# A fixed order up to the first channel-mixing output, and the scores of a head pair in one run

## The chip, the core and the metric

The kernel runs on one core of a Trainium2 chip. The core's engines each take their own queue of instructions in order: TensorE (PE; matrix products and transposes, written to PSUM), VectorE (DVE), ScalarE (ACT) and GpSimd (POOL, which here only issues loads). SyncE (SP) issues the stores. The metric is the device time of one execution in microseconds (us); for the kernel before it is the median of 11 runs, 346.16 us.

## The reference

Inputs are float32: q, k, v of 8 batches x 8 heads x 576 positions x 64, and four weight matrices. First comes sliding-window attention with a bias linear in distance, then an MLP mixer over its output.

```python
rel  = pos[:, None] - pos[None, :]
mask = (rel >= 0) & (rel < 128)
scores = where(mask, q @ k.T / sqrt(64) - slope[h] * abs(rel), -1e9)
x = softmax(scores) @ v                 # heads side by side: (8, 576, 512)
h = maximum(x.T @ w_tok1, 0) @ w_tok2   # token mixing: 576 -> 256 -> 576
u = x + h.T
out = u + maximum(u @ w_ch1, 0) @ w_ch2 # channel mixing: 512 -> 1536 -> 512
```

Each query sees itself and the 127 positions before it, so only the diagonal blocks of scores and their neighbours are computed.

## The kernel before

**Attention** goes by head pairs: g counts them over all batches, four to a batch, 0 to 31. A pair has three steps.

- `att_T(g)`: twelve transposes (L201) from the regrouped copies qg and kg into one PSUM tile tT, then a copy of q by ScalarE (L210) and of k by VectorE (L211) into qT and kT. For batch 0 (`early`) both copies are ScalarE's.
- `att_S(g, half)`: score products of half of the key blocks into a PSUM tile sp (L233: four matmuls in half 0, six in half 1, each using 64 of the array's 128 rows), two exponentials by ScalarE into pe (L241), and one product with the mask by VectorE into pb (L245).
- `att_V(g)`: eighteen matmuls with v into a PSUM tile ot (L267; v has a column of ones, which gives the sum), a reciprocal rt (L274) and the scaled copy into xb (L275).

tT, sp and ot share the PSUM pool `ps_at`, which has two buffers of two banks each. pe has three buffers, pb nine.

`regroup(b, h0, h1)` (L142) reorders the loaded q and k of a batch on VectorE, into qg and kg. It reads qn and kn, which `dma_qk` loads through POOL's queue, and it must come before the batch's `att_T`. The regroup of batch b+1 is called at the end of `att_T` of batch b's last pair (from batch 1 on), followed by `dma_qk(b + 3)`. `att_V` of a batch's last pair issues the loads of v for batch b+2.

**The mixer** of a batch has five steps. `tok1` is two groups of five matmuls (t, L310), with ScalarE's ReLU r1t (L315). `tok2` is five groups of two (ht, L323), with VectorE's addition ub (L327). `trans_u` is four groups of five transposes (ut, L336 and L340), with VectorE's copies UT (L345). `ch1` is 24 tiles ct of four matmuls (L351), each with ScalarE's ReLU into R2 (L356). `ch2` is four or five output chunks of twelve matmuls (o2, L379), cut into three parts of four; VectorE adds ub (L391) or copies (L387), and SP stores. All of these use the PSUM pool `ps_ma`, which has four buffers of one bank.

**The order.** `mixer_items(b, lead)` lists the work of mixer b together with the ch2 chunks of batch b-1: `lead` chunks stand before `tok1`, one behind it, one between the parts of `tok2`, the rest around `trans_u`. Every item has a cost written by hand. `spread(main, side)` calls the main items in order and puts the side items among them in proportion to these costs; `att_step(g)` gives the side items T(g+2), S(g+1) twice, V(g).

Three stretches follow each other:

1. Attention of batch 0, in an order written out by hand (`tc.manual_schedule()`: it holds for all engines).
2. Mixer 0, spread with attention of batch 1 (`att_step` from g = 2 on, limited to g >= 4 by `g0`; since it reaches ahead, T(8), T(9) and S(8) fall in here too) and with the first three ch2 chunks of batch 0 (`lead=3`, n1 = 9 parts). Here and after it, only TensorE's order is as called (`engines={ENG.PE}`). For the other engines the framework's scheduler sets the order. `regroup(1, 0, H)` is called as a side item of cost 0, behind the first twelve of the ch1 tiles of mixer 0.
3. Mixers 1 to 8, each spread with the attention of the batch after it.

The functions and the main part:

Of the kernel before, what the change touches and what calls it, by code (L numbers as in the profile page):

```python
# [9 lines left out]
ACT = mybir.ActivationFunctionType  # L10
ALU = mybir.AluOpType
ENG = mybir.EngineType
# [26 lines left out]
def kernel(  # L39
# [11 lines left out]
    nc = tc.nc  # L51
    P = nc.NUM_PARTITIONS
    B, H, S, D = q.shape
# [3 lines left out]
    scale = 1.0 / math.sqrt(D)  # L57
    slopes = [2.0 ** (-8.0 * (h + 1) / H) for h in range(H)]
    bf16 = mybir.dt.bfloat16
    f32 = mybir.dt.float32  # L60

    assert (S, D, H, B % 2) == (576, 64, 8, 0)
    NF = S // P
    TAIL = S - NF * P
    NCH = NF + 1
    W0 = S - P
    NHP = H // 2
    NDH = DTOK // P
    NCB = DM // P
    NHT = DCH // P  # L70
# [7 lines left out]
    pepool = ctx.enter_context(tc.tile_pool(name="pe", bufs=3))  # L78
    pbpool = ctx.enter_context(tc.tile_pool(name="pb", bufs=9))
# [5 lines left out]
    ps_at = ctx.enter_context(tc.tile_pool(name="ps_at", bufs=2, space=bass.MemoryType.PSUM))  # L85
# [21 lines left out]
    biascol = const.tile([P, H], f32, name="biascol")  # L107
# [3 lines left out]
    masks = const.tile([P, 2, H, 512], bf16, name="masks")  # L111


    def dma_qk(b, h0, h1):
        for raw, src in ((qn, q), (kn, k)):
            nc.gpsimd.dma_start(
                out=raw[b % 2][:RP, h0:h1, :],
                in_=src[b, h0:h1, :, :].rearrange("h (p j) d -> p h (j d)", j=TPP),
            )
# [70 lines left out]
    pbs = {}  # L190
# [23 lines left out]
            if b + 3 < B:  # L214
                dma_qk(b + 3, 0, H)

    def att_S(g, half):
        b, hp = divmod(g, NHP)
        qt, kt = qT[g % NR], kT[g % NR]
        sp = ps_at.tile([P, 2, 512], f32, name="sp", tag="at")  # L220
        for i in range(2):
            kb = 2 * half + i
            lastp = kb == NF - 1
            w = P + TAIL if lastp else 2 * P

            mms = [(0, w, kb * P, kb * P)]
            if lastp:
                mms.append((w, 2 * P, W0, NF * P))
            for x0, x1, k0, q0 in mms:

                for hh in range(2):
                    r = slice(hh * D, (hh + 1) * D)
                    nc.tensor.matmul(  # L233
                        sp[:, hh, i * 256 + x0 : i * 256 + x1],
                        lhsT=kt[r, k0 : k0 + P], rhs=qt[r, q0 : q0 + x1 - x0],
                        start=True, stop=True,
                    )
        pe = pepool.tile([P, 2, 512], bf16, name="pe", tag="pe")
        for i in range(2):
            h = 2 * hp + i  # L240
            nc.scalar.activation(  # L241
                out=pe[:, i, :], in_=sp[:, i, :], func=ACT.Exp, bias=biascol[:, h : h + 1], scale=scale,
            )
        pb = pbpool.tile([P, 2, 512], bf16, name="pb", tag="pb")
        nc.vector.tensor_tensor(  # L245
            out=pb[:, :, :], in0=pe[:, :, :],
            in1=masks[:, half, 2 * hp : 2 * hp + 2, :], op=ALU.mult,
        )
        pbs[g, half] = pb

    def att_V(g):
        b, hp = divmod(g, NHP)
# [34 lines left out]

    NG = B * NHP

    def att_step(g, g0=0):  # L290

        its = []
        if g0 <= g + 2 < NG:
            its.append((0.6, lambda: att_T(g + 2)))
        if g0 <= g + 1 < NG:
            its.append((0.5, lambda: att_S(g + 1, 0)))
            its.append((0.5, lambda: att_S(g + 1, 1)))
        if g0 <= g < NG:
            its.append((0.6, lambda: att_V(g)))
        return its  # L300

# [95 lines left out]
    def mixer_items(b, lead=1):  # L397

        chunks = []
        if b > 0:  # L400
            cs = list(range(NF)) if (b - 1) % 2 == 0 else [NF] + list(range(NF))
            chunks = [ch2_items(b - 1, c) for c in cs]
        its = []
        for _ in range(lead if chunks else 0):
            its += chunks.pop(0)
        if b < B:
            its += [(1.07, lambda dh=dh: tok1(b, dh)) for dh in range(NDH)]
            if chunks:
                its += chunks.pop(0)
            mid = chunks.pop(0) if chunks else []  # L410
            for c in range(NCH):
                its.append((0.43, lambda c=c: tok2(b, c)))
                if mid and c % 2 == 0:
                    its.append(mid.pop(0))
            its += mid
            last = chunks.pop() if chunks else []
            for ch in chunks:
                its += ch
            its += last[:1]
            for cb in range(NCB):  # L420
                its.append((0.25, lambda cb=cb: trans_u(b, cb)))
            its += last[1:]
            for ht_i in range(NHT):
                for x in range(2):
                    its.append((0.48, lambda ht_i=ht_i, x=x: ch1(b, ht_i, x)))
        else:
            for ch in chunks:
                its += ch
        return its


    with tc.manual_schedule():
        for i in range(2):
            nc.vector.memset(vp[i][:, :, :, D : D + 1], 1.0)
            nc.vector.memset(vp[i][0 : P - TAIL, NF, :, 0:D], 0.0)
        nc.vector.memset(W1[0 : P - TAIL, NF, :], 0.0)
        nc.vector.memset(patT[0 : P - TAIL, :], 0.0)
        dma_qk(0, 0, 2)
        nc.gpsimd.iota(
            row[:, :], pattern=[[1, P]], base=0, channel_multiplier=0,  # L440
            allow_small_or_imprecise_dtypes=True,
        )
        nc.gpsimd.iota(
            pidx, pattern=[[0, 1]], base=0, channel_multiplier=1,
            allow_small_or_imprecise_dtypes=True,
        )
        for hp in range(1, NHP):
            dma_qk(0, 2 * hp, 2 * hp + 2)
        dma_v_tail(0)
        for h in range(H):  # L450
            dma_v_head(0, h)
        nc.gpsimd.dma_start(
            out=W1[:, 0:NF, :], in_=moe_w_tok1[0 : NF * P, :].rearrange("(c p) d -> p c d", p=P)
        )
        nc.gpsimd.dma_start(out=W1[P - TAIL : P, NF, :], in_=moe_w_tok1[NF * P : S, :])
        nc.gpsimd.dma_start(
            out=W2[:, :, :], in_=moe_w_tok2.rearrange("(j p) s -> p j s", p=P)
        )
        for n in range(3):
            cs = slice(n * DCH // 3, (n + 1) * DCH // 3)  # L460
            nc.gpsimd.dma_start(
                out=WC1[:, :, cs], in_=moe_w_ch1[:, cs].rearrange("(j p) h -> p j h", p=P)
            )
        dma_qk(1, 0, H)
        nc.gpsimd.dma_start(
            out=WC2[:, :, :], in_=moe_w_ch2.rearrange("(j p) c -> p j c", p=P)
        )
        dma_v_tail(1)
        for c in range(NF):
            dma_v(1, c)  # L470


        build_consts()
        regroup(0, 0, 2)
        build_bias()
        att_T(0, True)
        build_masks(0)
        regroup(0, 2, 4)
        att_S(0, 0)
        att_T(1, True)  # L480
        build_masks(1)
        att_S(0, 1)
        regroup(0, 4, 6)
        att_S(1, 0)
        att_T(2, True)
        build_masks(2)
        att_S(1, 1)
        regroup(0, 6, 8)
        if B > 2:
            dma_qk(2, 0, H)  # L490
        att_S(2, 0)
        att_T(3, True)
        build_masks(3)
        att_S(2, 1)
        att_V(0)
        att_S(3, 0)
        att_V(1)
        att_S(3, 1)
        att_V(2)
        att_V(3)  # L500
        nc.vector.tensor_copy(out=swap[:, 0:TAIL], in_=ident[:, TAIL:P])
        nc.vector.tensor_copy(out=swap[:, TAIL:P], in_=ident[:, 0:TAIL])

    def run(its):
        for _, f in its:
            f()

    with tc.manual_schedule(engines={ENG.PE}):

        its0, its1 = mixer_items(0), mixer_items(1, lead=3)  # L510
        n0, n1 = len(its0) - NHT, 9
        run(its0[:n0])
        side = [(0.0, lambda: regroup(1, 0, H))]
        if B > 3:
            side.append((0.0, lambda: dma_qk(3, 0, H)))
        for g in range(NHP - 2, 2 * NHP):
            side += att_step(g, NHP)
        spread(its0[n0:] + its1[:n1], side)
        side = []
        for g in range(2 * NHP, 3 * NHP):  # L520
            side += att_step(g)
        spread(its1[n1:], side)
        for b in range(2, B + 1):
            side = []
            for g in range(NHP * (b + 1), NHP * (b + 2)):
                side += att_step(g)
            spread(mixer_items(b), side)
# [30 lines left out]
```

The softmax here doesn't subtract the row's maximum and nothing guards it: scores larger than these inputs give would overflow.

## Time and profile before

| | us |
|---|---|
| median of 11 runs (lowest, highest) | 346.16 (343.89, 348.07) |
| profiled execution: its time | 346.83 |
| its span, first to last instruction | 345.0 |
| TensorE matmuls busy | 306.7 (89%) |
| VectorE busy | 180.4 (52%) |
| ScalarE busy | 179.0 (52%) |
| GpSimd busy | 59.1 (17%) |
| mean of one: exponential L241 / ReLU L356 | 0.696 / 0.425 |
| mean of one: mask product L245 / regroup copy of a batch L142 | 0.689 / 0.95 |

Rows of a timeline give start, duration, engine, line, operation, out<-in with shapes, count, and in brackets the idle time before it with what ended it. A duration reaches from start to the end of the writes, and the next instruction on the same engine can start before that; what one costs in a row of many is the distance of starts. Rows of a waits view give engine, line and tile, what it waited for, us in total, times and the longest. Slices cut the span in 40; a digit is the busy share in tenths.

### The profile page before, as it was taken

Reading aid. Unit: us, or ns where it says so; the run is one execution under the profiler, and the core shown is the slowest. Engines: PE = TensorE matmul, PEld = TensorE weight load, DVE = VectorE, ACT = ScalarE, POOL = GpSimd, SP = SyncE. Lnnn points to the kernel's source line nnn. Section 1 sums busy time; section 2 is a strip of 40 time slices with the busy share of each in tenths; the row PEclk is TensorE's granted clock in tenths of the full one; section 3 lists DMA queues with packets and bytes.
Section 4 is the critical chain, followed back from the end, with each engine's and each line's share of the span. In section 5 each row is a group of like instructions: output and inputs, shape, how many; then the busy total and the mean of one; then the engine's idle time right before and its main releaser. Section 6 shows DMA issues by size and latency. Waiting matters only on the chain.

```text
span 345.0 us, 6712 instructions
## 1 busy us (share of the span) xinstructions
PE 306.7 (89%) x2816; PEld 189.3 (55%) x2816; DVE 180.4 (52%) x342; ACT 179.0 (52%) x373; POOL 59.1 (17%) x79
## 2 busy tenths in 40 slices
PE   2570689997789999999999999999999999999995
PEld 1350257553377545765567546764576456746742
DVE  6861452774864478434952396346932573335012
ACT  3850139854449643784369533855396427612800
POOL 8963150104100410022100400040000000000000
PEclk9999999998989999999999999999999999999999
DMA  7999999699190849109750902075000210011022
GB/s 89 136 171 205 199 165 148 85 195 99 33 137 2 56 75 194 39 4 98 118 112 2 99 32 86 7 49 83 33 32 2 61 61 32 2 61 63 0 63 92
DMA packets 59502, 27.76 MB, mean 80 GB/s; under 512 B 38672, under 2 KB 54864, under 8 KB 59472
## 3 DMA queue, kind: packets, MB, share of 16 engines
q0 software_dynamic: 54224, 17.90, 53.5%
q1 hardware_dynamic: 5248, 9.44, 8.2%
q8 instruction: 22, 0.36, 0.5%
q14 instruction: 8, 0.07, 0.1%
HBM read 35.78 MB, written 9.44 MB: 131 GB/s over the span
## 4 chain that ended last, share of the span: by engine, by line
PE 74%; DVE 10%; DMA 6%; POOL 3%; ACT 3%; issue 2%; ACTq 0%; POOLq 0%
PE ct L351 27%; PE o L379 24%; PE t L310 6%; DMA kn<-in_k_dram 6%; PE sp L233 4%; PE ot L267 4%; PE tT L201 3%; DVE ub L327 3%; PE ht L323 2%; PE ut L340 2%; DVE kg L142 2%; ACT pe L241 2%; POOL vp L134 2%; DVE kT L211 1%; DVE xb L275 1%
## 5 line engine op out<-in xcount | busy, mean ns | idle before, releaser
L379 PE MATMUL o<-WC,R 128*128 128x512 bf16 x432 | 104.2, 379 | 0.0
L351 PE MATMUL ct<-UT,WC 128*128 128x288 bf16 x768 | 104.1, 286 | 0.2
L241 ACT ACTIVATE pe<-sp,biascol 128x512 bf16<-128x512 f32 x128 | 81.3, 696 | 29.4 <-PE sp L233 29.4
L356 ACT ACTIVATE R<-ct 128x288 bf16<-128x288 f32 x192 | 73.7, 425 | 31.9 <-PE ct L351 25.6
L351 PEld LDWEIGHTS <-WC 128*128 128x128 bf16 x768 | 71.4, 98 | 22.1 <-issue 3.5
L245 DVE TENSOR_TENSOR pb<-pe,masks 128x1024 bf16<-128x1024 bf16 x64 | 44.1, 689 | 59.5 <-ACT pe L241 59.5
L379 PEld LDWEIGHTS <-R 128*128 128x128 bf16 x432 | 39.0, 98 | 41.7 <-issue 1.6
L210 ACT COPY qT<-tT 128x576 bf16<-128x576 bf16 x32 | 20.5, 641 | 55.4 <-PE tT L201 54.6
L128 POOL DMA_DIRECT2D vp<-in_v_dram x28 | 24.6, 890 | 122.8 <-PE ot L267 108.6
L211 DVE COPY kT<-tT 128x576 bf16<-128x576 bf16 x28 | 21.1, 755 | 38.3 <-ACT qT L210 38.3
L267 PE MATMUL ot<-vp,pb 128*128 128x65 bf16 x576 | 24.6, 200 | 11.3 <-DVE pb L245 9.5
L391 DVE TENSOR_TENSOR obt<-o,ub 128x512 f32<-128x512 f32 x32 | 22.0, 686 | 21.1 <-PE o L379 21.0
L267 PEld LDWEIGHTS <-pb 128*128 128x128 bf16 x576 | 23.1, 102 | 16.2 <-DVE pb L245 9.7
L233 PE MATMUL sp<-qT,kT 64*128 64x256 bf16 (+2 forms) x320 | 27.2, 269 | 3.1 <-ACT kT L211 1.2
L327 DVE TENSOR_TENSOR ub<-ht,xb 128x512 bf16<-128x512 f32 x40 | 25.6, 679 | 5.8 <-PE ht L323 5.8
L275 DVE TENSOR_TENSOR xb<-ot,rt 128x640 bf16<-128x640 f32 x32 | 26.3, 823 | 1.0
L315 ACT ACTIVATE r1t<-t 128x512 bf16<-128x512 f32 x16 | 9.6, 600 | 31.9 <-PE t L310 31.9
L310 PE MATMUL t<-xb,W 128*128 128x512 bf16 x80 | 22.1, 419 | 4.1 <-DVE xb L275 4.1
L233 PEld LDWEIGHTS <-kT 64*128 64x128 bf16 x320 | 11.4, 97 | 23.2 <-issue 18.7
L323 PE MATMUL ht<-r1t,W 128*128 128x512 bf16 x80 | 21.5, 379 | 1.6 <-DVE ub L327 1.1
L201 PE MATMUL tT<-ident,qg 96*128 96x96 bf16 x192 | 14.6, 216 | 9.1 <-DVE qg L142 9.1
L201 PEld LDWEIGHTS <-qg 96*128 96x128 bf16 x192 | 12.2, 102 | 14.9 <-DVE qg L142 10.5
(48 smaller groups left out, 166.7 us busy)
## 6 DMA issues: line engine op xcount, KB each, us to landing
out_dram<-obt SPq DMA_DIRECT2D x32, 256.0 KB, 2.0
qn<-in_q_dram POOLq DMA_DIRECT2D x7, 576.0 KB, 6.8
kn<-in_k_dram POOLq DMA_DIRECT2D x7, 576.0 KB, 10.1
vp<-in_v_dram POOLq DMA_DIRECT2D x28, 128.0 KB, 5.1
WC<-in_moe_w_ch_dram POOLq DMA_DIRECT2D x3, 512.0 KB, 10.7
WC<-in_moe_w_ch_dram POOLq DMA_DIRECT2D x1, 1536.0 KB, 23.6
vp<-in_v_dram POOLq DMA_DIRECT2D x16, 64.0 KB, 5.1
out_dram<-obt SPq DMA_DIRECT2D x8, 128.0 KB, 2.7
```

Source lines behind the costliest of these rows:

```text
L201: nc.tensor.transpose(tt[n][:, j * RP : (j + 1) * RP], t_raw[:RP, j, 2 * hp : 2 * hp + 2, :].rearrange("p h d -> p (h d)"), ident[:RP, :RP],)
L233: nc.tensor.matmul(sp[:, hh, i * 256 + x0 : i * 256 + x1], lhsT=kt[r, k0 : k0 + P], rhs=qt[r, q0 : q0 + x1 - x0], start=True, stop=True,)
L241: nc.scalar.activation(out=pe[:, i, :], in_=sp[:, i, :], func=ACT.Exp, bias=biascol[:, h : h + 1], scale=scale,)
L245: nc.vector.tensor_tensor(out=pb[:, :, :], in0=pe[:, :, :], in1=masks[:, half, 2 * hp : 2 * hp + 2, :], op=ALU.mult,)
L267: nc.tensor.matmul(ot[:, i, qb * (D + 1) : (qb + 1) * (D + 1)], lhsT=pb[:, i, col : col + P], rhs=vb[:, kc, h, :], start=(n == 0), stop=(n ...
L275: nc.vector.tensor_tensor(out=xb[b][:, :, 2 * hp * D : (2 * hp + 2) * D].rearrange("p c (i d) -> p i c d", i=2), in0=o4[:, :, :, 0:D], in1 ...
L310: nc.tensor.matmul(t1[:, :], lhsT=W1[:, c, dh * P : (dh + 1) * P], rhs=xb[b][:, c, :], start=(c == 0), stop=(c == NCH - 1),)
L323: nc.tensor.matmul(ht[:, :], lhsT=W2[:, j, c0(c) : c0(c) + P], rhs=r1s[b, j][:, :], start=(j == 0), stop=(j == NDH - 1),)
L327: nc.vector.tensor_tensor(out=ubs[b][:, c, :], in0=ht[:, :], in1=xb[b][:, c, :], op=ALU.add)
L351: nc.tensor.matmul(ct[:, :], lhsT=WC1[:, cb, ht_i * P : (ht_i + 1) * P], rhs=UT[:, cb, o : o + SH], start=(cb == 0), stop=(cb == NCB - 1),)
L356: nc.scalar.activation(out=R2[:, ht_i, o : o + SH], in_=ct[:, :], func=ACT.Relu)
L379: nc.tensor.matmul(o2[0][:, :], lhsT=R2[:, ht_i, col : col + P], rhs=WC2[:, ht_i, :], start=(ht_i == 0 and c != NF), stop=(ht_i == NHT - 1),)
```

## The change

There are four edits.

1. The hand-written, all-engine order now reaches on through mixer 0, attention of batch 1 and the first ch2 chunks of batch 0. `regroup(1, 0, H)` is called where it was, but VectorE now takes it in that place: behind the ub and UT of mixer 0.
2. In that stretch the side items are T and S of head pairs 4 to 7 alone, then all four V together at the end (`outputs=False`, `g1`).
3. `lead=2` and n1 = 6: two ch2 chunks of batch 0 stand before `tok1` of mixer 1, and two are left for mixer 1. T(8), T(9) and S(8) move into mixer 1 as well.
4. `att_S(g, halves)` does the matmuls of both halves first (both sp buffers), then the four exponentials and two mask products. `att_step` gives it one cost of 0.8. Batch 0's attention calls it with one half at a time, as before.

```diff
-    def att_S(g, half):
+    def att_S(g, halves=(0, 1)):
         b, hp = divmod(g, NHP)
         qt, kt = qT[g % NR], kT[g % NR]
-        sp = ps_at.tile([P, 2, 512], f32, name="sp", tag="at")
-        for i in range(2):
+        sps = {}
+        for half in halves:
+            sp = sps[half] = ps_at.tile([P, 2, 512], f32, name="sp", tag="at")
+            for i in range(2):
...
-        pe = pepool.tile([P, 2, 512], bf16, name="pe", tag="pe")
-        for i in range(2):
-            h = 2 * hp + i
-            nc.scalar.activation(
-                out=pe[:, i, :], in_=sp[:, i, :], func=ACT.Exp, bias=biascol[:, h : h + 1], scale=scale,
-            )
...
-        pbs[g, half] = pb
+        for half in halves:
+            pe = pepool.tile([P, 2, 512], bf16, name="pe", tag="pe")
+            for i in range(2):
+                h = 2 * hp + i
+                nc.scalar.activation(
+                    out=pe[:, i, :], in_=sps[half][:, i, :], func=ACT.Exp,
+                    bias=biascol[:, h : h + 1], scale=scale,
+                )
...
+            pbs[g, half] = pb
...
-    def att_step(g, g0=0):
+    def att_step(g, g0=0, g1=NG, outputs=True):
 
         its = []
-        if g0 <= g + 2 < NG:
+        if g0 <= g + 2 < g1:
             its.append((0.6, lambda: att_T(g + 2)))
-        if g0 <= g + 1 < NG:
-            its.append((0.5, lambda: att_S(g + 1, 0)))
-            its.append((0.5, lambda: att_S(g + 1, 1)))
-        if g0 <= g < NG:
+        if g0 <= g + 1 < g1:
+            its.append((0.8, lambda: att_S(g + 1)))
+        if g0 <= g < g1 and outputs:
             its.append((0.6, lambda: att_V(g)))
         return its
...
-    with tc.manual_schedule(engines={ENG.PE}):
-
-        its0, its1 = mixer_items(0), mixer_items(1, lead=3)
-        n0, n1 = len(its0) - NHT, 9
-        run(its0[:n0])
+        its0, its1 = mixer_items(0), mixer_items(1, lead=2)
+        n0, n1 = len(its0) - NHT, 6
+        for _, f in its0[:n0]:
+            f()
         side = [(0.0, lambda: regroup(1, 0, H))]
         if B > 3:
             side.append((0.0, lambda: dma_qk(3, 0, H)))
         for g in range(NHP - 2, 2 * NHP):
-            side += att_step(g, NHP)
+            side += att_step(g, NHP, 2 * NHP, outputs=False)
+        side += [(0.6, lambda g=g: att_V(g)) for g in range(NHP, 2 * NHP)]
         spread(its0[n0:] + its1[:n1], side)
-        side = []
+
+    with tc.manual_schedule(engines={ENG.PE}):
+        side = att_step(2 * NHP - 2, 2 * NHP) + att_step(2 * NHP - 1, 2 * NHP)
         for g in range(2 * NHP, 3 * NHP):
             side += att_step(g)
         spread(its1[n1:], side)
```

## The prediction

> **What bounds the kernel now.** I read the page's busy shares first, then the slices, then who waits for whom on TensorE, then three stretches of the timeline. Busy shares and slices:
>
> ```profile
> PE 306.7 (89%) x2816; PEld 189.3 (55%) x2816; DVE 180.4 (52%) x342; ACT 179.0 (52%) x373; POOL 59.1 (17%) x79
> PE   2570689997789999999999999999999999999995
> DMA  7999999699190849109750902075000210011022
> ```
>
> TensorE is at nines from about 100 us to the end: there every microsecond of its work or waiting is a microsecond of the kernel. Its 38 us of idle lie almost all before. The waits of TensorE:
>
> ```profile
> PE ot L267 <- DVE pb L245: 9.5, 1, 9.5
> PE tT L201 <- DVE qg L142: 9.1, 4, 5.2
> PE ut L336 <- DVE ub L327: 5.1, 2, 3.7
> PE t L310 <- DVE xb L275: 4.1, 2, 2.1
> ```
>
> The largest is one wait of 9.5 us on pb. VectorE's timeline at that place says what pb waited for:
>
> ```profile
> 23.27 0.82 DVE L275 TENSOR_TENSOR xb<-ot,rt 128x640 bf16<-128x640 f32 x1
> 33.46 0.96 DVE L142 COPY qg<-qn 96x3072 bf16<-96x3072 bf16 x1 [9.36 <-DMA qn<-in_q_dram]
> 34.34 0.68 DVE L245 TENSOR_TENSOR pb<-pe,masks 128x1024 bf16<-128x1024 bf16 x1
> ...
> 36.35 0.95 DVE L142 COPY kg<-kn 96x3072 bf16<-96x3072 bf16 x1
> 37.23 0.81 DVE L275 TENSOR_TENSOR xb<-ot,rt 128x640 bf16<-128x640 f32 x1
> 38.04 0.17 DVE L502 COPY swap<-ident 128x64 bf16<-128x64 bf16 x1
> ```
>
> The regroup of batch 1 (qg, kg) stands in VectorE's queue ahead of batch 0's last pb and last xb, and waits for loads that land at about 33.4 and 36.3. So batch 0's token mixing starts at 38.09 instead of right after its attention. Last, a piece of a channel-mixing stage, TensorE and then ScalarE:
>
> ```profile
> 138.92 0.39 PE L233 MATMUL sp<-qT,kT 64*128 64x256 bf16 x4
> 139.24 1.64 PE L351 MATMUL ct<-UT,WC 128*128 128x288 bf16 x12
> 140.82 0.40 PE L233 MATMUL sp<-qT,kT 64*128 64x256 bf16 x6
> 141.14 2.13 PE L351 MATMUL ct<-UT,WC 128*128 128x288 bf16 x16
> ```
>
> ```profile
> 139.35 1.27 ACT L241 ACTIVATE pe<-sp,biascol 128x512 bf16<-128x512 f32 x2 [1.98 <-PE sp L233]
> 140.51 1.01 ACT L356 ACTIVATE R<-ct 128x288 bf16<-128x288 f32 x3
> 141.38 1.30 ACT L241 ACTIVATE pe<-sp,biascol 128x512 bf16<-128x512 f32 x2
> 142.52 1.36 ACT L356 ACTIVATE R<-ct 128x288 bf16<-128x288 f32 x4
> ```
>
> TensorE never stops here: two exponentials hold ScalarE 1.16 us (139.35 to 140.51), so one takes 0.58; three R copies 0.87, so 0.29 each; a ct tile is four matmuls at 0.1225, 0.49 us, and four ct tiles fit in their pool.
>
> **The Trainium skill.** "TensorEngine Tiling (Array Packing)", Key Properties, says that changing the tiling mode drains TensorE. The trace agrees: twelve ct matmuls take 1.58 us to the next start when scores (64 rows) follow, 1.47 by 0.1225 each: 0.10 on entry. Four score matmuls are two pairs of 256 columns, about 0.22 by ct's rate, and take 0.32: 0.10 on exit (0 at least; I take 0.10). "TensorE: Matmul & The Clock Gate", Part 1, says that the clock halves after an idle window of about 3.4 us and returns after a busy one, the windows running freely. The trace agrees: the stretches 80 to 90 and 90 to 100 us had a mean granted clock of 0.83, around the idle at 79.1 to 81.2 and 92.6 to 96.3. "Perfetto Trace Analysis", Identifying Performance Opportunities, takes a gap that repeats on the saturated engine as too few buffers for the next tile; before, no ct waits in these stages.
>
> **Part 1, the regroup behind batch 0's mixer copies.** In the built program VectorE now has pb, xb, xb, the five ub and four UT, and only then qg and kg of batch 1. From before's rows: the last exponentials end at 24.84; pb 24.9 to 25.5; V(2)'s reciprocal and xb to 26.6; V(3)'s (0.25 + 0.82) to 27.67. Token mixing starts at 27.7, not 38.09: **-10.4**. Its weights were issued at 14.2 and 15.8 and landed 4.3 and 6.1 later; the last channel weights landed at about 31.4, and the first ct comes near 37. The next 9.3 us repeat. UT ends near 37.9, so qg and kg run to 39.6 (kn there at 36.3) under the first 13 ct tiles; their first reader is due at 43.95. The DMA queue is full until 63 us whatever the kernel does, so landings stay.
>
> **Part 2, batch 1's scores and V in a fixed order with two ch2 chunks.** From 43.95 I walked the three queues with before's durations. TensorE waits: for kT before the second half of scores 4 to 7, 0.35 + 1.1 + 0.55 + 0.6 (both score buffers are wanted at once, and the one that T used is free only when kT is copied); for xb before V(6), 0.6; before token mixing 1, 1.65: 4.85 in all, where before had 3.6 (0.2, 0.6, 0.45, 0.35, 2.0). Four merges give 0.8 back. Batch 2's regroup now follows T(7) near 56; its loads, issued at 34.02 and 36.89 with 19.2 and 19.4 to land, are there at 53.2 and 56.3: just in time. Token mixing 1 starts near 66.25. Before, it started at 81.15, but had done three ch2 parts (2.6), two T (1.0) and one S (0.85) more: 76.7. So 10.4 earlier still: **0**.
>
> **Part 3, mixer 1** now carries those parts. VectorE's chain ends it: ub(4) near 81.8, then xb 0.75, obt 0.6, kT 0.67, qg and kg of batch 3 (1.74, now ahead of UT), UT 1.55: 87.1. ct starts near 86.75 and one score run (0.65) comes later: 87.4 against 99.07, 11.7 earlier; about 0.3 of that is lost to a half-clock window that now holds ct. **-1.0** more.
>
> **Part 4, both halves in one run, head pairs 13 to 31.** A merge saves one entry and one exit, 0.20. But ScalarE now gets four exponentials in a row, and the R copies stand behind them. From the start of a score run: first exponential at 0.43 (138.92 to 139.35), four to 2.75, one R of 0.42 to 3.17, hop 0.05. TensorE has 0.54 of scores and four ct tiles, 1.96, and stands from 2.50 to about 3.2: 0.70. Minus the merge, +0.50 for each run that has four ct tiles straight behind it: two in each of mixers 2 to 5 and one in mixer 6, 9 x 0.50 = **+4.5**. In mixer 1 a V (0.55) lies among the four: 0.15 less 0.20, nothing. The other 10 runs lie among ch2 parts, which hold one buffer for 2.6 us: 10 x -0.20 = **-2.0**. In mixers 2 and 4 the score half that filled the wait for ub(1) has moved behind it (before: 0.34 at 129.74): the wait grows by 0.55, **+1.1**. In 3 and 5 the run stays ahead of it.
>
> Sum: -10.4 + 0 - 1.0 + 4.5 - 2.0 + 1.1 = **-7.8**: span 345.0 to 337.2. The profiled execution took 346.83, 1.83 around its span and 0.67 above the median 346.16; on the median that is **338.4**.
>
> **Bounds.** Stall per run: 0 (if ScalarE catches up better) to 1.0, so -6.3 to +2.7. Half-clock windows: one spared (-1.7) to one more, or a later warm-up of the first token mixing (+1.7). Walk of part 2: -1 to +2.5. VectorE's and ScalarE's later orders are also rearranged by the scheduler, about 1 either way.
>
> **Rivals.**
> A, the runs of exponentials are hidden: R and ct need no more buffers than they have. For it: ScalarE is busy 52%. Against: one queue, four buffers, 2.32 us. -10.4 - 1.0 - 27 x 0.2 (two merges of mixer 1 included) + 1.1: about 330.5 on the median; 0.10.
> B, half of part 1 is taken by the loads: kn of batch 2 landing 3 us later holds VectorE before pb(6), or the wait before token mixing 1 grows. For it: kg has 0.4 us of margin. Against: nothing of that queue moves. About 342; 0.17.
> C, slower: the two score buffers. Each run wants both at once, so T's copies and the V before it must be over; if TensorE stands 0.7 us before or behind each of the 28 runs, not the 9, that is 28 x 0.5 = 14 against 11.4: about 349. It decides from 0.41 net per run. For it: the four waits in part 2. Against: from mixer 2 on, 1.9 us or more lie between T and S, and the copies take 1.5. 0.07.
> D, the change does nothing that lasts: the stages before 100 us were off the end. Against: TensorE has no idle after 100 to absorb it. 0.04, about 346.
>
> My forecast holds 0.62, its own range 335.5 to 341.5. To hold 8 in 10 I reach into A and B: 333.5 to 343.5. A half per cent, about what a measurement of this kernel can tell, is 1.7 us: faster (below 344.4) 0.86, within 0.06, slower 0.08.
>
> **What would show it.** Right: token mixing 0 starts near 28 with no wait of 9 us on pb; token mixing 1 near 66; a new wait "ct on ScalarE's R" of 9 times some 0.7, about 6 us; ScalarE with pe in fours; scores of ten in one piece. Wrong: token mixing still past 35 (part 1); no wait on R (A); regroup of batch 2 waiting for kn (B); waits on every sp (C). The forecast fails most easily in the size of the stall, which counts nine times, and in the half-clock windows, which the phase of an execution moves.

## The result, and the profile after

The changed kernel takes 339.25 us in the median (338.41 to 340.94, 12 runs). The kernel before takes 346.44 us over all its runs (343.73 to 348.07, 47 runs). The ratio is 0.98, with a 95% interval of 0.9782 to 0.9818: about 7 us faster. The prediction was 338.4, in a range of 333.5 to 343.5. The profiled execution took 338.41 us, the shortest of the twelve, with a span of 336.6 (before: 346.83 and 345.0).

The waits of TensorE after (engine, line and tile; what it waited for; us in total, times, longest):

```profile
PE tT L201 <- DVE qg L142: 8.5, 3, 5.2
PE ct L354 <- ACT R L359: 4.7, 9, 0.5
PE t L313 <- DVE xb L279: 2.6, 2, 1.4
PE sp L235 <- DVE kT L211: 2.4, 6, 0.9
PE ct L354 <- DVE UT L348: 2.3, 1, 2.3
PE ht L326 <- DVE ub L330: 2.3, 2, 1.1
```

The one wait of 9.5 us on pb is gone. New are the waits of ct on R, nine times, and of ct on UT, once. The waits of ht on ub were three of 0.3 to 0.4 and are now two of 1.1 each. The busy share and the clock of the same page:

```profile
PE 302.5 (90%) x2816; PEld 191.6 (57%) x2816; DVE 178.3 (53%) x342; ACT 179.2 (53%) x373; POOL 59.3 (18%) x79
PEclk9999999999999999999999999999999999999999
```

Ahead of 32.4 us this trace has no record of the clock, and the digits there tell nothing.

VectorE's timeline where the long wait was. The last pb of batch 0 now follows its exponentials, and qg and kg stand behind the UT copies:

```profile
25.02 0.69 DVE L249 TENSOR_TENSOR pb<-pe,masks 128x1024 bf16<-128x1024 bf16 x1 [0.77 <-ACT pe L244]
27.02 0.82 DVE L279 TENSOR_TENSOR xb<-ot,rt 128x640 bf16<-128x640 f32 x1
...
37.04 1.55 DVE L348 COPY UT<-ut 128x576 bf16<-128x576 bf16 x4 [0.55 <-PE ut L343]
38.51 0.95 DVE L142 COPY qg<-qn 96x3072 bf16<-96x3072 bf16 x1
39.38 0.95 DVE L142 COPY kg<-kn 96x3072 bf16<-96x3072 bf16 x1
```

And a channel-mixing stage of mixer 2, TensorE and then ScalarE, which answers to the stage shown of before:

```profile
126.19 0.65 PE L354 MATMUL ct<-UT,WC 128*128 128x288 bf16 x4
126.77 0.61 PE L235 MATMUL sp<-qT,kT 64*128 64x256 bf16 x10
127.32 2.13 PE L354 MATMUL ct<-UT,WC 128*128 128x288 bf16 x16
129.98 1.14 PE L354 MATMUL ct<-UT,WC 128*128 128x288 bf16 x8 [0.53 <-ACT R L359]
```

```profile
127.21 2.42 ACT L244 ACTIVATE pe<-sp,biascol 128x512 bf16<-128x512 f32 x4
129.50 2.07 ACT L359 ACTIVATE R<-ct 128x288 bf16<-128x288 f32 x6
```

Sixteen ct matmuls are issued from 127.32 and would end at 129.28, at 0.1225 each; the next one starts at 129.98. The stall is 0.70 us of issue time. The view gives 0.53, since it counts from the end of the last write. The first R behind the four exponentials starts at 129.50 and frees the buffer.

Where the time went shows in the starts of token mixing, mixer by mixer (first t of each, us). The column of differences is after less before.

| mixer | before | after | after less before |
|---|---|---|---|
| 0 | 38.09 | 27.89 | -10.2 |
| 1 | 81.15 | 66.92 | -14.2 (4.5 of it work moved into mixer 1) |
| 2 | 118.68 | 105.66 | -13.0 |
| 3 | 157.02 | 145.34 | -11.7 |
| 4 | 193.20 | 182.10 | -11.1 |
| 5 | 231.54 | 221.78 | -9.8 |
| 6 | 267.42 | 258.54 | -8.9 |
| 7 | 302.86 | 294.44 | -8.4 |
| end of the span | 345.0 | 336.6 | -8.4 |

13.0 us are ahead by mixer 2, and 4.6 of them are given back between the starts of mixer 2 and mixer 7: 184.18 us before, 188.78 after.

### The profile page after: what moved, and what is told of

Read it like the earlier page. It is cut to its first block, busy times and chain, and to the rows that moved or that the text cites. A ratio compares the mean times of both kernels' runs of the same rounds, so it can differ in the third digit from the quotient of the medians.

```text
span 336.6 us, 6715 instructions
## 1 busy us (share of the span) xinstructions
PE 302.5 (90%) x2816; PEld 191.6 (57%) x2816; DVE 178.3 (53%) x342; ACT 179.2 (53%) x373; POOL 59.3 (18%) x79
## 4 chain that ended last, share of the span: by engine, by line
PE 66%; ACT 13%; DVE 13%; issue 5%; DMA 2%; POOL 1%; POOLq 0%; DVEq 0%; ACTq 0%
PE ct L354 22%; PE o L382 22%; ACT pe L244 10%; PE t L313 6%; PE ot L271 4%; PE tT L201 4%; PE sp L235 3%; PE ht L326 3%; DVE pb L249 2%; DVE ub L330 2%; DVE xb L279 2%; DMA kn<-in_k_dram 2%; DVE kg L142 1%; PE ut L343 1%; DVE qg L142 1%
## 5 line engine op out<-in xcount | busy, mean ns | idle before, releaser
L354 PEld LDWEIGHTS <-WC 128*128 128x128 bf16 x768 | 72.3, 98 | 30.0 <-issue 10.6
L244 ACT ACTIVATE pe<-sp,biascol 128x512 bf16<-128x512 f32 x128 | 77.6, 692 | 19.6 <-PE sp L235 19.6
L382 PEld LDWEIGHTS <-R 128*128 128x128 bf16 x432 | 39.9, 98 | 42.3
L235 PE MATMUL sp<-qT,kT 64*128 64x256 bf16 (+2 forms) x320 | 23.3, 264 | 4.3 <-DVE kT L211 2.4
L313 PE MATMUL t<-xb,W 128*128 128x512 bf16 x80 | 21.2, 410 | 2.6 <-DVE xb L279 2.6
L235 PEld LDWEIGHTS <-kT 64*128 64x128 bf16 x320 | 13.3, 97 | 17.2 <-issue 12.8
```

The lines of the kernel that those rows point to most:

```text
L235: nc.tensor.matmul(sp[:, hh, i * 256 + x0 : i * 256 + x1], lhsT=kt[r, k0 : k0 + P], rhs=qt[r, q0 : q0 + x1 - x0], start=True, stop=True,)
L244: nc.scalar.activation(out=pe[:, i, :], in_=sps[half][:, i, :], func=ACT.Exp, bias=biascol[:, h : h + 1], scale=scale,)
L313: nc.tensor.matmul(t1[:, :], lhsT=W1[:, c, dh * P : (dh + 1) * P], rhs=xb[b][:, c, :], start=(c == 0), stop=(c == NCH - 1),)
L354: nc.tensor.matmul(ct[:, :], lhsT=WC1[:, cb, ht_i * P : (ht_i + 1) * P], rhs=UT[:, cb, o : o + SH], start=(cb == 0), stop=(cb == NCB - 1),)
L382: nc.tensor.matmul(o2[0][:, :], lhsT=R2[:, ht_i, col : col + P], rhs=WC2[:, ht_i, :], start=(ht_i == 0 and c != NF), stop=(ht_i == NHT - 1),)
```

## The experiments

The theory was: part 1 brings about 10 us; the order of parts 2 and 3 adds little; part 4 gives some of it back, since R copies wait behind four exponentials, and since VectorE's regroup stands among the additions of token mixing. The main rivals: merging the score halves is itself a gain (A), TensorE stands for the two score buffers (C), the loads limit part 1 (B). Medians within one group of runs share their runs of the kernel before: 346.26 us for the first four kernels, 347.09 for the last four. So a difference between the medians of kernels from different groups is uncertain by about 0.8 us.

### Part 1 alone

```diff
+    its0, its1 = mixer_items(0), mixer_items(1, lead=3)
+    n0, n1 = len(its0) - NHT, 9
+
+    with tc.manual_schedule():
+        run(its0[:n0])
+        regroup(1, 0, H)
+
     with tc.manual_schedule(engines={ENG.PE}):
-
-        its0, its1 = mixer_items(0), mixer_items(1, lead=3)
-        n0, n1 = len(its0) - NHT, 9
-        run(its0[:n0])
-        side = [(0.0, lambda: regroup(1, 0, H))]
+        side = []
```

In the traces TensorE's and ScalarE's orders are those of before; VectorE's differs in the place of one regroup (its two copies) and in nothing else.

> The kernel before with part 1 alone: mixer 0 up to its first twelve ch1 tiles, and then the regroup of batch 1, stand in the all-engine order; TensorE's order and all else as before. My theory (part 1 is worth 10.4 us and the loads of batch 2 are just in time): token mixing 0 starts near 27.9, token mixing 1 near 71, and the median is about 336 to 337. Rival (the loads take part of it back): the regroup of batch 2 waits for kn by 2 us or more, and the median is above 338.5. Rival (most of the change's gain comes from parts 2 and 3): the median is above 341.

Measured: 336.37 us (335.18 to 337.47), ratio 0.9714 (0.9687 to 0.974). Token mixing 0 starts at 27.55 and token mixing 1 at 70.80, 10.5 and 10.35 earlier than before, and the lead stays to the end (span 334.7 against 345.0). The regroup of batch 2 does not wait for kn there (VectorE's timeline):

```profile
54.29 0.68 DVE L245 TENSOR_TENSOR pb<-pe,masks 128x1024 bf16<-128x1024 bf16 x1
54.91 0.96 DVE L142 COPY qg<-qn 96x3072 bf16<-96x3072 bf16 x1
55.78 0.95 DVE L142 COPY kg<-kn 96x3072 bf16<-96x3072 bf16 x1
56.65 0.75 DVE L211 COPY kT<-tT 128x576 bf16<-128x576 bf16 x1
```

So one change of place on VectorE is worth more than the whole change, and rival B did not happen.

### The whole change without part 4

```diff
-            its.append((0.8, lambda: att_S(g + 1)))
+            its.append((0.5, lambda: att_S(g + 1, (0,))))
+            its.append((0.5, lambda: att_S(g + 1, (1,))))
```

> The changed kernel with part 4 undone: each half of a score run is its own side item again (cost 0.5 each), parts 1 to 3 stay. My theory (part 4 costs 0.5 in each of nine runs and about 1 in two token-mixing waits, and gives 0.2 back elsewhere): no wait of ct on R, and a median of about 335.5 to 337, 2 to 4 us below the changed kernel. Rival (merging is a gain and what was given back is something else): the median is 340 or more.

Measured: 334.89 us (333.39 to 335.58), ratio 0.9662 (0.9635 to 0.969), 4.4 us below the changed kernel. That is a little below what was expected. No wait of ct on R is left, ht waits 0.33, 0.39 and 0.33, and mixers 2 to 7 take 184.18 us between their starts, as before. Part 4 is a loss where it stands, and beside the 4.6 us there it costs 0.9 earlier: from the first ct of mixer 0 to token mixing 1 it takes 28.37 us here and 29.24 in the changed kernel. The medians show less than that sum, since these executions mostly have one stretch of half clock more (mean clock 0.988, the changed kernel's 0.995; see the last section). Against part 1 alone this kernel, which adds parts 2 and 3, is 1.5 us faster.

### Part 4 alone

The new `att_S` and its one side item, in the kernel before (batch 0 calls one half at a time).

> The kernel before with part 4 alone: matmuls, then exponentials, of both halves in one run; the regroup, the lead and the V's as before. My theory: ct waits on R about nine times by 0.5 to 0.7 us, the 9.5 us wait on pb stays, and the median is 348 to 351, 2 to 4 us above the kernel before. Rival (both halves together gain by the saved drains): the median is 341 to 344.

Measured: 352.81 us (352.3 to 354.26), ratio 1.02 (1.0173 to 1.0227): 6.5 us slower than before. The direction is the theory's, the size is outside what I expected. Its waits:

```profile
PE ot L271 <- DVE pb L249: 9.3, 1, 9.3
PE ut L339 <- DVE ub L330: 5.7, 2, 4.4
PE ct L354 <- ACT R L359: 4.7, 9, 0.5
PE sp L235 <- DVE kT L211: 3.5, 7, 1.1
```

From the start of mixer 2 to that of mixer 7 it takes 188.78 us, the same as the changed kernel: 4.6 more than before. The other 1.5 us of its span are there when mixer 2 starts (120.15 against 118.68), and two places make them. From the first ct of mixer 0 to token mixing 1 it is 0.9 (34.67 us against 33.80): there TensorE waits five times for kT before a second half (0.21, 0.92, 1.15, 0.33, 0.33). That is the cost of wanting two buffers at once among batch 1's transposes. My expectation had left it out, though the prediction's walk of part 2 has it. Another 0.7 is in the first token mixing, ahead of all merged runs: it ran longer at half clock, and ct starts 10.0 us behind t in place of 9.3. So the merge explains about 5.5 of the 6.5.

### The exponentials of the second half apart

Both halves' matmuls stay in one run; the second half's exponentials and mask product become a side item behind it. `att_S` is divided for this: `att_M` does the matmuls of both halves, `att_E` the exponentials and mask product of one.

```diff
...
-            its.append((0.8, lambda: att_S(g + 1)))
+
+            def both(g=g):
+                att_M(g + 1)
+                att_E(g + 1, 0)
+            its.append((0.8, both))
+            its.append((0.2, lambda: att_E(g + 1, 1)))
```

> The changed kernel with the score matmuls of both halves still in one run (both buffers wanted at once, one drain), but the exponentials and mask product of the second half made a side item of their own (cost 0.2) behind it, so that ScalarE's queue takes R copies between them. My theory (the stall is R behind four exponentials): the waits of ct on R fall from 0.52 each to 0.1 or less, and the median is 333 to 335.5. Rival (TensorE stands because a run wants both score buffers): the waits stay or move to sp, and the median is within 1 us of 339.25.

Measured: 332.14 us (331.75 to 333.1), ratio 0.9599 (0.9575 to 0.9623), 7.1 us below the changed kernel, and lower than expected. It is 2.8 below the kernel with halves apart by the medians, and 1.9 by the spans of the two profiles, which have one stretch of half clock each. TensorE and ScalarE in the same stage:

```profile
126.64 0.61 PE L236 MATMUL sp<-qT,kT 64*128 64x256 bf16 x10
127.19 3.12 PE L368 MATMUL ct<-UT,WC 128*128 128x288 bf16 x24
130.14 0.71 PE L280 MATMUL ot<-vp,pb 128*128 128x65 bf16 x18
```

```profile
127.08 1.26 ACT L248 ACTIVATE pe<-sp,biascol 128x512 bf16<-128x512 f32 x2
128.23 0.41 ACT L373 ACTIVATE R<-ct 128x288 bf16<-128x288 f32 x1
128.52 0.70 ACT L248 ACTIVATE pe<-sp,biascol 128x512 bf16<-128x512 f32 x1
129.09 0.73 ACT L373 ACTIVATE R<-ct 128x288 bf16<-128x288 f32 x2
```

R copies now pass between the exponentials, and 24 ct matmuls run through. TensorE still takes both score buffers in one run, so rival C is out as the cause of the nine stalls: it was ScalarE's order. (The added side item moves some main items too, so TensorE's order is not the same throughout; in the stage shown it is.) And with the stall away the merge is a gain, as A had it: mixers 2 to 7 take 181.99 us between their starts, 2.2 less than before.

### The regroup of the next batch called later

The call moves from the end of a batch's fourth transposes to the end of the score run of its third pair, which comes behind them.

```diff
...
-        if hp == NHP - 1 and 0 < b < B - 1:
-            regroup(b + 1, 0, H)
-            if b + 3 < B:
-                dma_qk(b + 3, 0, H)
+
+    def next_regroup(b):
+        regroup(b + 1, 0, H)
+        if b + 3 < B:
+            dma_qk(b + 3, 0, H)
 
     def att_S(g, halves=(0, 1)):
...
+        if hp == NHP - 2 and 0 < b < B - 1:
+            next_regroup(b)
```

> The changed kernel with one call moved: the regroup of the next batch (and the loads behind it) is called at the end of the score run of a batch's third pair, which stands behind the transposes of its fourth, and no longer right behind these transposes. VectorE then has UT before qg and kg in mixer 1, and ub(1) behind qg alone in mixers 2 and 4; TensorE's order is the same. My theory (part 3's wait for UT of 2.3 us and the two token-mixing waits of 1.14 us come from the regroup in VectorE's queue): the wait for UT falls to about 0.6, the two waits to about 0.3, and the median falls by 2.5 to 3.5 us to about 336 to 337. Rival (they come from ht's own work and the score half that moved away): the waits stay and the median is within 1 us of 339.25.

Measured: 334.27 us (334.14 to 334.99), ratio 0.9645 (0.9623 to 0.9666), 5.0 us below the changed kernel, more than the 2.5 to 3.5 expected. First the changed kernel's VectorE in token mixing 2, then the same with the call moved:

```profile
113.16 0.68 DVE L330 TENSOR_TENSOR ub<-ht,xb 128x512 bf16<-128x512 f32 x1
113.75 0.95 DVE L142 COPY qg<-qn 96x3072 bf16<-96x3072 bf16 x1
114.62 0.95 DVE L142 COPY kg<-kn 96x3072 bf16<-96x3072 bf16 x1
115.49 0.75 DVE L211 COPY kT<-tT 128x576 bf16<-128x576 bf16 x1
116.16 2.47 DVE L330 TENSOR_TENSOR ub<-ht,xb 128x512 bf16<-128x512 f32 x4
```

```profile
112.06 0.95 DVE L142 COPY qg<-qn 96x3072 bf16<-96x3072 bf16 x1
112.93 0.68 DVE L333 TENSOR_TENSOR ub<-ht,xb 128x512 bf16<-128x512 f32 x1
113.53 0.74 DVE L211 COPY kT<-tT 128x576 bf16<-128x576 bf16 x1
114.19 1.87 DVE L333 TENSOR_TENSOR ub<-ht,xb 128x512 bf16<-128x512 f32 x3
115.99 0.95 DVE L142 COPY kg<-kn 96x3072 bf16<-96x3072 bf16 x1
```

In the changed kernel the second ub waits for both regroup copies and kT; with the call moved, for qg alone. The two waits of 1.14 us disappear, and so does most of the one on UT (2.32 to 0.59). In the starts of token mixing that is 1.7 us of mixer 1 (37.01 in place of 38.74) and 2.6 from mixer 2 to 7 (186.18 in place of 188.78), and the span is those 4.3 us shorter. The rest of the 5.0 goes with the clock: no timed execution of this kernel shows a whole half-clock stretch, while eleven of the changed kernel's twelve do (last section); below the one that does not, 338.41, it is 4.1. The nine waits on R are still there, 0.5 each, and TensorE's and ScalarE's orders are the changed kernel's, so the two causes are separate.

### Both

> The kernel with the exponentials of the second half apart, and the regroup of the next batch called later as well. If the two causes are independent, the two gains add: about 332.1 less 2 to 3.5 us, 328.5 to 330.5. If they share a cause (VectorE and ScalarE made free by the same waits), it stays within 1 us of 332.1.

Measured: 328.19 us (327.88 to 328.34), ratio 0.946 (0.944 to 0.948). It is 3.95 below the kernel with the exponentials apart, a little more than expected. The two gains add, but for about 1 us: alone they are 7.1 and 5.0, together 11.1, and 0.8 us of difference can come from comparing across groups. Part of what is shared is known: with the exponentials apart the waits of ht on ub had already fallen from 1.14 to 0.76. This is the fastest kernel of the study: 5.4% below the kernel before, 11 us below the changed one.

### All engines as called

```diff
-    with tc.manual_schedule(engines={ENG.PE}):
+    with tc.manual_schedule():
```

> The kernel with the exponentials of the second half apart, with all engines' orders as called to the end of the program instead of TensorE's alone. If the scheduler's orders of VectorE and ScalarE cost something that part 4's bounds (1 us either way) took in, this is 0.5 to 1.5 us below 332.1; if they are as good as the called ones, it is within 0.7 us; if the scheduler's are better, above 333.

Measured, against the kernel with the exponentials apart: 335.96 us (335.58 to 336.46), ratio 0.9685 (0.9664 to 0.9707), in place of 332.14. All of the 3.8 us lie between the starts of mixers 2 and 7 (185.82 against 181.99). The waits of ht on ub in mixers 2 and 4 become 1.69 us (0.76 there), and the waits of ut on UT in mixers 3 and 5 become 1.24 (0.33 there). So a fixed order is no good in itself: from mixer 1 on the scheduler's orders are the better ones, except for the regroup's place. VectorE's and ScalarE's orders both changed here and were not tried apart; the grown waits are on VectorE.

### V among transposes and scores again

The kernel with halves apart, with `outputs=True` and no V appended at the end.

> The kernel with the halves apart (parts 1 to 3 without part 4), with the V of batch 1 back among its T and S as before, so that of parts 2 and 3 only the moved T, S and ch2 chunks are left. Prediction's walk (putting the V together is worth nothing): a median within 0.7 us of the 334.9 of the kernel with halves apart. Rival (the V together are what gained 1.5 us over the regroup alone): 336 to 337.

Measured: 335.18 us (334.58 to 336.44), ratio 0.9667 (0.9641 to 0.9693), against 0.9662 (0.9635 to 0.969) with the V together. By the medians there is no difference, but that is the clock's doing. Of these four executions three have one half-clock stretch and one has two (mean clock 0.993 and 0.988); with the V together two have one and three have two. With one stretch the V among take 334.58 to 335.33 us and the V together 333.39 and 333.78; with two it is 336.44 against 334.89 to 335.58. In the profiles it takes 29.28 us against 28.37 from the first ct of mixer 0 to token mixing 1, all at full clock. Scores wait for xb twice there (0.74 and 0.97), and not at all with the V together.

So the V together bring about 1 of the 1.5 us of parts 2 and 3. What the moved transposes, scores and chunks bring is too little to tell from noise here. The prediction had put both at nothing.

## Why the prediction held, step by step

**Part 1: right.** Predicted -10.4; token mixing 0 starts at 27.89 in place of 27.7, so -10.2, and -10.3 at the end of the span where part 1 stands alone. No load took it back.

**Part 2: right within 0.7.** Token mixing 1 was put at 66.25 and starts at 66.92. The waits that the walk named are there: 0.21, 0.92, 0.38 and 0.45 before second halves, 0.44 before V(6), 1.42 before token mixing. They make 3.8 in place of its 4.85; from the first transposes to token mixing 1 it took 22.27 us all the same, against 22.3 in the walk, so about 1 us lies elsewhere, which was not followed. The 0.67 is mostly the first token mixing, where ct starts 9.8 us behind t in place of the 9.3 that the sum took over. It ran longer at half clock: the ten t take 4.42 us, and 3.90 before, and the record of full clock begins 4.5 us behind the first t (27.89 to 32.42) in place of 3.2 (38.09 to 41.33). The walk puts waits and merges together at nothing; the kernel with halves apart shows that the merge by itself costs 0.9 us in this stretch.

**Part 3: too small.** Predicted 11.7 earlier at the first ct of mixer 1, with 0.3 of it lost, so 11.4; mixer 2 starts 13.0 earlier. Part 3 is therefore 2.8 in place of 1.0. The first ct starts at 84.81, but its four matmuls wait for the UT copies one by one (84.81, 85.17, 85.54, 85.90), as good as a start at 85.54; with the score run of 0.65 behind it that is 12.9 ahead of 99.07. The term that was mis-sized is the clock. The profile before has two half-clock stretches in mixer 1, at 82.29 to 85.70 and 95.94 to 99.35; the walk took over before's durations in the first (five t took 2.33 there, 1.24 after) and kept the second at ct, and the profiled execution after has neither. That is an accident of this execution, since eleven of the twelve have one or two. The wait of ct on UT is as described, and it was shown by moving the call:

```profile
81.32 0.68 DVE L394 TENSOR_TENSOR obt<-o,ub 128x512 f32<-128x512 f32 x1
81.92 0.74 DVE L211 COPY kT<-tT 128x576 bf16<-128x576 bf16 x1
82.58 0.94 DVE L142 COPY qg<-qn 96x3072 bf16<-96x3072 bf16 x1
83.45 0.95 DVE L142 COPY kg<-kn 96x3072 bf16<-96x3072 bf16 x1
84.31 1.53 DVE L348 COPY UT<-ut 128x576 bf16<-128x576 bf16 x4
```

```profile
84.81 1.87 PE L354 MATMUL ct<-UT,WC 128*128 128x288 bf16 x8 [2.32 <-DVE UT L348]
```

**Part 4: the mechanism right, the stall to the hundredth, the sum 1 us too small.** The stall was put at 0.70 for nine runs; it is 0.70, nine times. A run costs 0.58 - 0.49 = 0.09 on entry and 0.55 by itself, 0.64 in place of 0.84 for two halves: the 0.20 of the sum. Together +3.6 was predicted from mixer 2 on, and +4.6 measured. What the sum lacked are waits outside the nine stalls. Mixers 2 and 4 gave +1.34 each in place of 1.15: the wait for ub grew from 0.34 to 1.14, not to 0.89. The step that failed is "the wait grows by 0.55": it counts the score half that moved away, and not that VectorE comes late as well. ub(0) starts 1.55 us behind its ht there (113.16 - 111.61) in place of 0.94 before (125.78 - 124.84). Right ahead of it stand the second pb, which now waits for four exponentials, and the V's copies. With the regroup's call moved the wait is gone although the score half stays away, so it takes the regroup between ub(0) and ub(1) to make it.

Mixer 5 gave +0.88, predicted +0.6. One of its score runs waits for kT before its second half (0.27 at 232.02), which the prediction had argued against from mixer 2 on. Mixer 3 has the same wait (155.58) and takes the same 36.77 us; that it gave +0.58, nearly as worked out, is luck, since a wait of 0.39 for ub that only before had (168.14) went away. Mixer 6 gave +0.46, predicted +0.1: 0.26 of it is the fourth ct matmul (277.48 in place of 277.23), which waits for the last UT copy, and that one now stands on VectorE behind two pb.

**The sum and the median.** -7.8 was predicted for the span and -8.4 measured: 13.0 in place of 11.4 by mixer 2, and 4.6 in place of 3.6 given back behind it. The two errors partly cancel, and that is luck. On the median the change is -7.2, since the profiled execution after had no half-clock stretch inside its work where most of the others had one, and the profiled one before lay 0.4 above its median.

**The rivals.** A fell as it was put: the runs of exponentials are not hidden. (Its sum counts 27 merges; by the prediction's own account there are 21 left, 19 in part 4 and two in mixer 1, which makes 331.7 in place of 330.5.) What it supposed, a gain from the saved drains, shows once they are apart (-2.2 from mixer 2 to 7). Whether more buffers for ct would hide the runs was not tried. B did not happen. C fell by the kernel with exponentials apart. What is left of it are the waits before second halves: in the first stages they are worth 0.9 us, with part 4 alone and in the changed kernel, and in mixers 3 and 5 there is one of 0.27 each. D fell with part 1 alone.

## What to carry to other kernels

When an in-order engine waits for a load, ask what useful work stands behind that instruction: moving the two regroup copies of one batch was worth 10 us, with no work removed. Before work is merged into longer runs on one engine, compare the longest run on the engine that drains the buffers with what these buffers hold: here four exponentials of 0.58 us against four tiles of 0.49. A merge that saves drains on TensorE and a bunching on ScalarE can be had apart, and then the gain stays without the loss. When medians lie within 1 or 2 us, compare executions of the same mean clock before calling two kernels equal.

## What the runs showed that I had not expected

Stretches of half clock set most of the spread between executions of the changed kernel and of the one before. Every such stretch that ends inside a span lasts 3.413 us or twice that. This is the length that the Trainium skill, "TensorE: Matmul & The Clock Gate", Part 1, gives for its free-running activity window. An execution's mean clock therefore tells their number: about 0.005 for each, and up to 0.002 for one that the end of the span cuts off. Of the changed kernel's 12 executions one has a mean clock of 0.999 (338.41 us), eight have 0.995 (338.91 to 339.69) and three 0.990 (340.43 to 340.94). So one stretch more costs about 1 us. The kernel before mostly has 0.990, and the one execution at 1.0 in the first group took 344.91 against a median of 346.26 beside it. Where the wait of 2.3 us on UT is gone (regroup called later, alone or with the exponentials apart) all nine executions have 0.998 to 1.0, and those of one kernel spread by less than 0.9 us.

The prediction said that the trace agrees with a halving after an idle window of about 3.4 us. It agrees in the length, but less idle time was enough. All whole stretches of the record, at full clock and at half, are multiples of 3.413 us, so they lie on a grid. The step of the grid ahead of before's first half-clock stretch, 78.87 to 82.29, holds only 2.0 us without a matmul. In the changed kernel's profile the wait on UT, 82.5 to 84.8, is cut by the grid at 83.62, and the clock stays full. That the phase of the grid decides fits this and is not shown: the traces give no sharp limit, since a step with 1.4 us without a matmul was followed by half clock (halves apart, 81.83 to 85.25) and one with 1.5 us was not (before, 44.74 to 48.15).
